# MLP 2's first pair all by Strassen's scheme, with VectorE's order written out and out tiles laid into their own batch's columns

## The chip, the cores and the metric

The kernel runs on one core of a Trainium2 chip. Its metric is the device time in microseconds. Before the change three runs took 769.46 to 769.73 us, median 769.64. An engine of the core works through its own queue in order: TensorE (matmuls, PE in the profile; its weight loads are PEld), VectorE (DVE), ScalarE (ACT), GpSimd (POOL) and SyncE (SP, which issues the DMAs). Engines wait for each other through semaphores.

## The reference, cut to what matters

Clustered attention feeds MLP 1 (512 to 2048 to 512, SiLU), and that feeds MLP 2, a gated one. The change is at the seam of the two MLPs.

```python
def _moe2_ref(x, w_gate, w_val, w_out):
    gate = 1.0 / (1.0 + np.exp(-(x @ w_gate)))
    val = x @ w_val
    return (gate * val @ w_out).astype(np.float32)
```

x has 1536 tokens (2 batches of 768) and 512 columns; MLP 2's hidden width is 1536. Everything is float32.

## The kernel before, in words

**Precision.** Every float32 operand is split into two tiles of a rounder type, hi and lo: ScalarE casts the source to hi (`cast`, L65), then VectorE or GpSimd subtracts hi from the source into lo (L77 for activations, L773 for weights, L956 in `split` for gated products). A product is three matmuls: hi hi, hi lo, lo hi.

**MLP 2 by pairs.** The hidden width is cut into six pairs of 256 columns (`i` from 0 to 5). Each pair has a gate weight (w2g), a value weight (w2v) and an out weight (w2o), each loaded as two chunks. A chunk is fetched raw (tiles rg, rv, ru; two buffers in all, so a fetch waits until the chunk two before it has been read for the last time), then converted: two ScalarE passes (L730, L732; tiles cg, cv, cu), one GpSimd pass (L733), two VectorE passes (L741, L748). `come` issues fetch and first passes, `arrive` the rest.

**Strassen's scheme** (`strassen`). The activations of a batch are four quarters b11, b21, b12, b22 (two row halves by two token halves of 384), the weight four quarters as well. Seven products with sums of the quarters replace eight: x, y, z, w, v, and X and W, which accumulate onto the banks of x and w. Each is six matmuls of 384 columns for one batch. X needs that ScalarE has copied x out of its bank (L923). The sums of the activations are t1 to t4 (L91 to L102), formed by VectorE and then split; those of the weight are formed by GpSimd (L793 to L796).

**The first pair.** It is the seam: MLP 1's last out products (`mixed`, tiles y, batch 0 then batch 1) are added to acc by VectorE (L996) while TensorE is to go on. In before, batch 0 of pair 0 is multiplied directly (`gated_directly`, tiles q and r, eight products with plain quarters), batch 1 by the scheme, gate first, then value; then come all six out tiles of pair 0 (`out_of(0)`, tiles z). An out tile is two blocks of 128 tokens by 512 columns (12 matmuls of 512 columns); pair 0's are copied by ScalarE into acc (L994), the later ones are added by VectorE. acc also holds MLP 1's result, the source of the quarters, so a tile may overwrite only columns whose quarters have been used. Tile z of blocks t and u goes to acc's columns t and u; those don't belong to one batch alone.

**Order.** TensorE's order is written out (a manual schedule), VectorE's, ScalarE's and GpSimd's are set by the scheduler, held back in places by `issue_after` (list `behind`).

## Time and profile before

| what | value |
|---|---|
| median of 3 runs | 769.64 us |
| profiled execution, its own time | 769.74 us |
| its span | 768.0 us |
| TensorE busy | 757.5 us (99%) |
| VectorE, ScalarE, GpSimd busy | 592.3, 425.2, 386.0 us |
| chain that ended last | TensorE 90%, VectorE 4%, ScalarE 3%, DMA 2% |

A timeline row gives the start in us from the span's start, the length, the engine, the source line, the operation, the tile written and those read. A matmul's own length (0.33 us for 384 columns) is longer than the distance to the next one, since they are pipelined; a block's cost is read from start to start. MLP 1's last out products run from 471.2 to 487.84, pair 0 of MLP 2 from there to 535.53, pair 1 begins there. In a name like g_1x the g is the gate (v: the value), 1 the batch, x the product; buffer numbers are left out.

### The profile page before, as it was taken

The numbers are of one execution on the slowest core, as the hardware profiler recorded it, in microseconds if no ns is written. First come the engines' busy times: TensorE is split into PE (matmuls) and PEld (weight loads), VectorE is DVE, ScalarE is ACT, GpSimd is POOL, SyncE is SP. The second block draws the span as 40 slices with busy tenths as digits, with TensorE's granted clock in tenths as the row PEclk, the third lists the DMA queues.
The fourth block names the chain that finished last, engine by engine and source line by source line (L and its number), as shares of the span: only waits on it lengthen the run. The fifth ranks groups of instructions, "written<-read, shape, count | busy, mean of one in ns | idle before, by whom it ended". The sixth has DMA issues, their size and how long they took to land.

```text
span 768.0 us, 11449 instructions
## 1 busy us (share of the span) xinstructions
PE 757.5 (99%) x4302; PEld 650.9 (85%) x4302; DVE 592.3 (77%) x762; ACT 425.2 (55%) x736; POOL 386.0 (50%) x359
## 2 busy tenths in 40 slices
PE   7999999999999999999999999999999999999997
PEld 4766776677768998998989989998998989999896
DVE  6887887788787968798978577966596767858566
ACT  6777776776886662544615536747434525353320
POOL 5335134643655772566646546355546745564430
PEclk9999999999999999999999999999999999999999
DMA  7677457447122122132222120111112112211104
GB/s 201 175 210 193 114 149 196 120 125 200 34 77 81 57 82 83 55 111 82 83 83 83 55 83 10 47 56 55 55 56 100 66 56 84 79 57 56 55 0 165
DMA packets 25487, 71.60 MB, mean 93 GB/s; under 512 B 4484, under 2 KB 4952, under 8 KB 25432
## 3 DMA queue, kind: packets, MB, share of 16 engines
q1 hardware_dynamic: 24888, 70.84, 30.8%
q8 instruction: 34, 0.56, 0.3%
q14 instruction: 21, 0.17, 0.1%
q10 hardware_dynamic: 544, 0.03, 0.0%
HBM read 48.01 MB, written 3.19 MB: 67 GB/s over the span
## 4 chain that ended last, share of the span: by engine, by line
PE 90%; DVE 4%; ACT 3%; DMA 2%; issue 1%; POOL 0%; SPq 0%; ACTq 0%; POOLq 0%; DVEq 0%
PE z L1078 12%; PE s L469 8%; PE v L519 7%; PE t L506 5%; PE y L1017 4%; PE h_0w L899 4%; PE h_0x L899 4%; PE g_0w L899 3%; PE g_0x L899 3%; PE v_0x L899 2%; PE v_0w L899 2%; PE y_00None L1017 2%; PE y_01None L1017 2%; PE y_20None L1017 2%; PE y_11None L1017 2%; PE y_10None L1017 2%
## 5 line engine op out<-in xcount | busy, mean ns | idle before, releaser
L482 ACT ACTIVATE e<-s,nm 128x768 f32<-128x768 f32 x96 | 86.4, 900 | 34.0 <-DVE nm L477 33.1
L477 DVE TENSOR_REDUCE nm<-s 128x1 f32<-128x768 f32 x96 | 91.4, 953 | 10.2 <-PE s L469 8.6
L1078 PE MATMUL z<-wu,ghb 128*128 128x512 f32 (+1 forms) x292 | 89.3, 387 | 0.7 <-DVE v_0u L913 0.7
L519 PE MATMUL v<-ph,vv 128*64 128x384 f32 x384 | 69.0, 494 | 0.2 <-DVE xf L531 0.2
L1078 PEld LDWEIGHTS z<-wu,ghb 128*128 128x128 f32 x292 | 54.4, 188 | 12.0 <-DVE v_0u L913 1.1
L469 PE MATMUL s<-ka,qa 128*128 128x384 f32 x192 | 57.5, 380 | 1.7 <-ACT e L482 1.3
L506 PE MATMUL t<-ident,e 128*128 128x128 f32 x384 | 58.5, 275 | 0.1
L996 DVE TENSOR_TENSOR acc<-z,acc 128x1024 f32<-128x1024 f32 (+2 forms) x32 | 37.0, 1157 | 26.7 <-PE z L1078 26.2
L1078 PE MATMUL z<-wu,glb 128*128 128x512 f32 (+1 forms) x146 | 56.5, 387 | 0.0
L506 PEld LDWEIGHTS t<-ident,e 128*128 128x128 f32 x384 | 44.9, 140 | 11.3 <-issue 9.0
L519 PEld LDWEIGHTS v<-ph,vv 128*64 128x64 f32 x384 | 24.7, 136 | 32.8 <-issue 29.0
L469 PE MATMUL s<-k,q 128*128 128x384 f32 x192 | 49.6, 339 | 0.0
L65 ACT ACTIVATE ph<-t 128x512 f32<-128x512 f32 x68 | 40.5, 597 | 12.4 <-PE t L506 11.8
L68 DVE COPY ph<-u 128x512 f32<-128x512 f32 x48 | 32.8, 683 | 16.3 <-PE u L496 16.3
L550 POOL TENSOR_TENSOR acc<-xf,rb 128x768 f32<-128x768 f32 x7 | 12.9, 1839 | 57.0 <-DMA rb<-d_rb 41.2
L773 POOL TENSOR_TENSOR wo<-co,wo 128x512 fp32r<-128x512 f32 x16 | 22.6, 1416 | 35.3 <-ACT wo L65 35.2
L773 POOL TENSOR_TENSOR wu<-cu,wu 128x512 fp32r<-128x512 f32 x12 | 15.5, 1295 | 42.1 <-ACT wu L65 42.1
L469 PEld LDWEIGHTS s<-k,q 128*128 128x128 f32 x192 | 34.5, 188 | 0.5 <-ACT k L339 0.3
L469 PEld LDWEIGHTS s<-ka,qa 128*128 128x128 f32 x192 | 28.9, 190 | 6.9 <-ACT e L482 6.0
L1017 PE MATMUL y<-gha,wo 128*128 128x384 f32 x128 | 32.8, 334 | 0.0
L1078 PEld LDWEIGHTS z<-wu,glb 128*128 128x128 f32 x146 | 27.4, 188 | 5.7 <-DVE glb L956 0.2
L531 DVE TENSOR_TENSOR xf<-v,other 64x384 f32<-64x384 f32 x32 | 17.7, 553 | 14.8 <-ACT other L528 14.3
(691 smaller groups left out, 2138.9 us busy)
## 6 DMA issues: line engine op xcount, KB each, us to landing
ri<-in_w1i SPq DMA_DIRECT2D x16, 512.0 KB, 3.2
ro<-in_w1o SPq DMA_DIRECT2D x16, 512.0 KB, 3.3
ka<-kh SPq DMA_DIRECT2D x32, 192.0 KB, 3.5
rg<-in_w2g SPq DMA_DIRECT2D x12, 512.0 KB, 4.1
rv<-in_w2v SPq DMA_DIRECT2D x12, 512.0 KB, 3.2
ru<-in_w2o SPq DMA_DIRECT2D x12, 512.0 KB, 3.2
qq<-in_qT SPq DMA_DIRECT2D x8, 384.0 KB, 3.4
kk<-in_kT SPq DMA_DIRECT2D x8, 384.0 KB, 4.2
```

The source lines that it names most:

```text
L65: return nc.scalar.activation(o, i, AF.Copy)
L68: return nc.vector.tensor_copy(o, i)
L469: nc.tensor.matmul(s[:, g, 0:HS], lhsT=a[:, j, i * P : (i + 1) * P], rhs=c[:, j, g * HS : (g + 1) * HS], start=n == 0, stop=n == 1,)
L477: maxima.append(nc.vector.tensor_reduce(nm, s[:, :, 0:HS], axis=AX.XY, op=ALU.max, negate=True))
L482: x = nc.scalar.activation(e, s[:, :, 0:HS], AF.Exp, bias=nm, scale=1.0, accum_out=tots[p][:, n : n + 1])
L506: nc.tensor.transpose(t[:, kt, :], e[:, kt * P : (kt + 1) * P], ident)
L519: m = nc.tensor.matmul(o[(L, U)[kt % 2]], lhsT=vv[:, j, kt, :], rhs=ring[:, kt, g * G : (g + 1) * G], start=n < 2, stop=n >= NT - 2,)
L773: nc.gpsimd.tensor_tensor(lo, src, hi, op=ALU.subtract)
L899: nc.tensor.matmul(o[:, b, 0:HS], lhsT=w[a][s][:, k, :], rhs=right[b, q][t][:, k, :], start=start and k == 0 and n == 0, stop=k == KQ - 1 ...
L996: added.append(nc.vector.tensor_tensor(z, o, z, op=ALU.add))
L1017: nc.tensor.matmul(o[:, d, 0:width], lhsT=s[:, d, k, :], rhs=t[:, c], start=k == 0 and m == 0, stop=k == 1 and m == 2,)
L1078: nc.tensor.matmul(o[:, a, c], lhsT=s[:, q * P : (q + 1) * P], rhs=r[:, c], start=k == 0 and m == 0, stop=k == 1 and m == 2, skip_group_ch ...
```

## The change

- Batch 0 of pair 0 goes by the scheme too. Gate and value products alternate in the order x X y z w v W (`together`), and ghb and glb of their products are split a little later (`late`).
- Out tiles of pair 0 are made of blocks of one batch and laid into that batch's columns (`place_of`), so three come after batch 0's products and three after batch 1's. In the later pairs a tile is made of the two batches' blocks. The rows stored at the end are reassembled by the store, from runs of 256 or 128 columns.
- From MLP 1's last out products to the end of batch 1's blocks VectorE's order is written out too. The conversions of w2o (pair 0), w2g and w2v (pair 1) are placed in it. ScalarE's sigmoid table is loaded by a tiny operation ahead of batch 0.

```diff
...
+    def scheme_operands(temporary, name, b, caster, adder):
+
+        b11, b21, b12, b22 = quarters(b).values()
+        sums = {}
+
+        def minus(n, x, y):
+            sums[n] = temporary(f"{name}t{n}{b}")
+            adder.tensor_tensor(sums[n], x, y, op=ALU.subtract)
+
+        def make(*which):
+            for w in which:
+                if w == "T1":
+                    minus("t1", b12, b11)
+                elif w == "T2":
+                    minus("t2", b22, sums["t1"])
+                elif w == "T3":
+                    minus("t3", b22, b12)
+                elif w == "T4":
+                    minus("t4", sums["t2"], b21)
+                elif w in sums:
+                    right_operand(name, b, w, sums[w], caster, adder)
+                else:
+                    right_quarter(name, b, w, caster, adder)
+
+        return make
...
+        if key[2:]:
+            chunk = result(coming[what, i].pop(0))
+            name = f"{what[1]}{i}"
+            if what == "2o":
+                made[place[key]] = two(chunk, f"u{i}_{key[2]}")
+            elif key[2]:
+                made[place[what, i]] = scheme(halves.pop(), chunk, name)
+            else:
+                halves.append(chunk)
...
-        for c in range(n, min(n + look[0] + 1, place["2o", 1, 0])):
+        for c in range(n, min(n + look[0] + 1, place["2o", 0, 0])):
...
-                if c == place["2g", 1]:
-                    behind.extend(multiplied[1:2] * 4 + multiplied[-1:] * 4)
...
+            parts = partial(split, g, m, (h, bs), f"b{i}", eng)
+            if together and eng is nc.vector:
+                late.append(parts)
+            else:
+                parts()
+
+        if together:
+            order = "xXyzwvW"
+            g = strassen(weights("2g", i), f"g{i}", gate, bs, order)
+            v = strassen(weights("2v", i), f"v{i}", value, bs, order)
+            for stage in (g, v) * 7:
+                next(stage)
+                yield
+            return
...
-    def gated_directly(i, b):
...
+    def place_of(t, u):
+
+        (h, b, r), (g, a, q) = t, u
+        if h != g:
+            return acc[:, :, :, b, half:].rearrange("p (g d) h s -> p g (d h) s", g=2)
+        if b == a:
+            return acc[:, 2 * h : 2 * h + 2, :, b, 0:half]
+        if r < 2:
+            return acc[:, 2 * h + r, :, :, 0:half].rearrange("p h b s -> p b h s")
+        return acc[:, 2 * h : 2 * h + 2, :, :, half:].rearrange("p d h b s -> p b (d h) s")
...
-        pairs = [(t, t + 1) for t in range(0, 2 * half, 2)]
         if i == 0:
-            ts = [t for b in range(B) for t in range(2 * half) if t % half // PER == b]
-            pairs = [tuple(ts[n : n + 2]) for n in range(0, 2 * half, 2)]
-        oc = oa.rearrange("p (t c) -> p t c", c=NB)
-        def products(o, t, u, k, rows=(0, 1), c=slice(0, NB)):
+            pairs = [p for b in range(B) for p in (((0, b, 0), (0, b, 1)), ((0, b, 2), (1, b, 2)), ((1, b, 0), (1, b, 1)))]
+        else:
+            pairs = [((h, 0, r), (h, 1, r)) for h in range(2) for r in ((0, 1, 2), (2, 0, 1))[h]]
...
+            accumulate(z, o.rearrange("p a (n w) -> p a n w", w=z.shape[-1]), i == 0)
...
+            nc.sync.dma_start(out[n : n + P, c].rearrange("t (n w) -> t n w", w=z.shape[-1]), z)
...
-    beside = plain_operands("y", 0)
-    steps(mixed(N1 - 1, 1), beside)
-    run(beside)
-    for q in ("11", "21", "22"):
-        right_quarter("y", 1, q, ACT, DVE)
-    run(sums("y", 1))
-    last("y", 1)
-    run(gated_directly(0, 0))
-    run(gated(0, ONE[1]))
-    run(sums("y", 0))
-    last("y", 0)
-    run(out_of(0))
+    come("2o", 0)
+    order.__exit__(None, None, None)
+    order = tc.manual_schedule(engines={mybir.EngineType.PE, mybir.EngineType.DVE})
+    order.__enter__()
+    zero, one = (scheme_operands(temporary, "y", b, ACT, DVE) for b in range(B))
+    rest = mixed(N1 - 1, 1)
+    zero("11", "21")
+    table = temporary("table")[:, 0, 0:1]
+    nc.scalar.activation(table, right[0, "21"][0][:, 0, 0:1].bitcast(F32), AF.Sigmoid)
+    zero("T1", "T2", "T3", "t2")
+    next(rest)
+    zero("t1", "T4")
+    next(rest)
+    next(rest)
+    zero("t3")
+    run(rest)
+    zero("t4")
+    arrive("2o", 0, 0)
+
+    def split_late():
+        while late:
+            late.pop(0)()
+
+    def both(b, between):
+        stages = gated(0, ONE[b], True)
+        for n in range(14):
+            next(stages)
+            if n in (4, 12, 13):
+                split_late()
+            for make, *what in between.get(n, ()):
+                make(*what)
+
+    both(0, {5: [(zero, "22")], 7: [(arrive, "2o", 0, 1), (come, "2g", 1)], 9: [(one, "11")]})
+    outs = out_of(0)
+    steps(outs, n=3)
+    one("21", "T1", "T2")
+    arrive("2g", 1, 0)
+    one("t2", "t1", "T3", "t3", "T4")
+    both(1, {5: [(one, "t4")], 7: [(one, "22")], 9: [(arrive, "2g", 1, 1), (come, "2v", 1)]})
+    order.__exit__(None, None, None)
+    order = tc.manual_schedule(engines={mybir.EngineType.PE})
+    order.__enter__()
+    arrive("2v", 1)
+    run(outs)
...
```

The instructions stand as follows in the built programs (line numbers of each kernel's own file; the number behind a name tells buffers apart).

TensorE, where batch 0 of pair 0 ends and batch 1 begins, before (r is the value of batch 0 formed directly, its six-matmul rows one per quarter):

```order
L966 MATMUL r_01_5384<-y_5195,wv0b 128x384 x6
L966 MATMUL r_01_5384<-y_5212,wv0b 128x384 x6
L966 MATMUL r_01_5384<-y_5229,wv0b 128x384 x6
L966 MATMUL r_01_5384<-y_5246,wv0b 128x384 x6
L899 MATMUL g_1x<-y_5249,wg0a 128x384 x6
L899 MATMUL g_1y<-yt_5262,wg0s 128x384 x6
L899 MATMUL g_1z<-yt_5272,wg0t 128x384 x6
L899 MATMUL g_1w<-yt_5275,wg0s 128x384 x6
L899 MATMUL g_1x<-y_5252,wg0a 128x384 x6
L899 MATMUL g_1v<-yt_5267,wg0b 128x384 x6
```

TensorE, the start of batch 0 now:

```order
L932 MATMUL g_0x<-y_5196,wg0a 128x384 x6
L932 MATMUL v_0x<-y_5196,wv0a 128x384 x6
L932 MATMUL g_0x<-y_5199,wg0a 128x384 x6
L932 MATMUL v_0x<-y_5199,wv0a 128x384 x6
L932 MATMUL g_0y<-yt_5210,wg0s 128x384 x6
L932 MATMUL v_0y<-yt_5210,wv0s 128x384 x6
L932 MATMUL g_0z<-yt_5260,wg0t 128x384 x6
L932 MATMUL v_0z<-yt_5260,wv0t 128x384 x6
L932 MATMUL g_0w<-yt_5227,wg0s 128x384 x6
L932 MATMUL v_0w<-yt_5227,wv0s 128x384 x6
```

The 16 rows of q and r have become 14 that alternate, and X comes two rows behind its x where it came four behind before.

ScalarE, around the copy of g_1x (the first product of batch 1), before:

```order
L1051 ACTIVATE g_1_0_5341<-q_01_5316 128x768
L65 ACTIVATE ghb_0_5380<-g_0_0_5314 128x2x384
L923 ACTIVATE g_1u_5415<-g_1x 128x384
L65 ACTIVATE ghb_1_5410<-g_1_0_5341 128x2x384
L65 ACTIVATE wg1d<-cg_1_5574 128x256
L65 ACTIVATE wg1a<-cg_0_5566 128x512
L1032 ACTIVATE g_001_5456<-g_1x 128x384
L730 ACTIVATE cv_0_5605<-rv_0_5603 128x512
L732 ACTIVATE rv_0_5603<-rv_0_5603 128x512
```

ScalarE there now (z_2 is the last out tile of batch 0; cv and rv are the passes over w2v's first chunk of pair 1, yt is the cast of t3 of batch 1):

```order
L65 ACTIVATE wg1a<-cg_0_5366 128x512
L1027 ACTIVATE acc<-z_2_5469 128x4x256
L756 ACTIVATE cv_0_5623<-rv_0_5621 128x512
L758 ACTIVATE rv_0_5621<-rv_0_5621 128x512
L65 ACTIVATE yt_5500<-ytt_5498 128x768
L956 ACTIVATE g_1u_5506<-g_1x 128x384
L956 ACTIVATE v_1u_5515<-v_1x 128x384
L1065 ACTIVATE g_001_5529<-g_1x 128x384
```

The two passes stood behind g_1x's copy and the sigmoid of its bank; now they and a cast stand ahead of the copy.

VectorE, where w2g's first chunk of pair 1 (cg_0) is converted, before (in before it runs beside batch 1's blocks):

```order
L1055 TENSOR_TENSOR g_0_0_5314<-r_00_5354,g_0_0_5314 128x768
L956 TENSOR_TENSOR glb_0_5381<-g_0_0_5314,ghb_0_5380 128x2x384
L1055 TENSOR_TENSOR g_1_0_5341<-r_01_5384,g_1_0_5341 128x768
L741 SCALAR_TENSOR_TENSOR cg_0_5566<-cg_0_5566,rg_0_5564 128x512
L741 SCALAR_TENSOR_TENSOR cg_1_5574<-cg_1_5574,rg_1_5572 128x512
L748 SCALAR_TENSOR_TENSOR cg_0_5566<-rg_0_5564,cg_0_5566 128x512
L913 TENSOR_TENSOR g_1u_5415<-g_1y,g_1u_5415 128x384
```

VectorE there now, at the end of batch 0 (glb and g_0u belong to batch 0's gated products, y and ytt to batch 1's operands):

```order
L989 TENSOR_TENSOR glb_1_5397<-g_0u_5341,ghb_1_5396 128x384
L946 TENSOR_TENSOR v_0u_5295<-v_0w,v_0u_5295 128x384
L1071 TENSOR_TENSOR g_0u_5286<-v_0u_5295,g_0u_5286 128x384
L989 TENSOR_TENSOR glb_0_5327<-g_0u_5286,ghb_0_5326 128x384
L77 TENSOR_TENSOR y_5483<-acc,y_5483 128x768
L113 TENSOR_TENSOR ytt_5486<-acc 128x768
L113 TENSOR_TENSOR ytt_5488<-acc,ytt_5486 128x768
L767 SCALAR_TENSOR_TENSOR cg_0_5366<-cg_0_5366,rg_0_5364 128x512
L774 SCALAR_TENSOR_TENSOR cg_0_5366<-rg_0_5364,cg_0_5366 128x512
```

The chunk's passes stand at the end of batch 0's work and of three operations for batch 1, and ahead of the rest of batch 1's operands.

## Rows read from the trace of the kernel before

**Rows 1.** The page: engine totals, and the granted clock over the span.
```profile
PE 757.5 (99%) x4302; PEld 650.9 (85%) x4302; DVE 592.3 (77%) x762; ACT 425.2 (55%) x736; POOL 386.0 (50%) x359
...
PEclk9999999999999999999999999999999999999999
```

**Rows 2.** Windows: length, busy us of PE, PEld, DVE, ACT, POOL, clock, DMA.
```profile
0.00:10.00 10.00, 7.23 (x30) 2.64 (x30) 6.10 (x43) 5.45 (x10) 2.92 (x10) 1.00 0.60 160
471.20:487.84 16.64, 16.64 (x97) 16.64 (x97) 15.75 (x18) 10.46 (x18) 8.89 (x9) 1.00 0.19 63
487.84:504.48 16.64, 16.64 (x97) 16.64 (x97) 13.99 (x16) 10.02 (x13) 3.48 (x3) 1.00 0.01 1
504.48:519.07 14.59, 14.59 (x85) 14.43 (x84) 9.90 (x17) 8.19 (x16) 10.36 (x11) 1.00 0.23 74
519.07:535.53 16.46, 16.46 (x73) 13.63 (x73) 12.61 (x18) 12.03 (x19) 7.50 (x7) 1.00 0.19 64
535.53:750.00 214.47, 214.10 (x1141) 201.85 (x1139) 150.19 (x153) 91.89 (x143) 114.18 (x114) 1.00 0.17 60
```

**Rows 3.** TensorE's timeline: start, length, engine, line, operation, tiles, count.
```profile
487.84 4.32 PE L966 MATMUL q<-y,wg0a 128*128 128x384 f32 x24
...
521.93 0.62 PE L1078 MATMUL z<-wu,ghb 128*128 128x512 f32 x2
...
524.65 0.62 PE L1078 MATMUL z<-wu,ghb 128*128 128x512 f32 x2
...
535.53 2.27 PE L899 MATMUL g_0x<-y,wg1a 128*128 128x384 f32 x12
```

**Rows 4.** Timeline of VectorE and GpSimd (fields as before).
```profile
478.14 0.95 DVE L77 TENSOR_TENSOR y<-acc,y 128x768 fp32r<-128x768 f32 x1
479.00 0.94 DVE L996 TENSOR_TENSOR acc<-y,acc 128x768 f32<-128x768 f32 x1
479.87 1.33 DVE L77 TENSOR_TENSOR y<-acc,y 128x768 fp32r<-128x768 f32 x1
...
505.56 1.28 DVE L741 SCALAR_TENSOR_TENSOR cg<-cg,rg 128x512 int32<-128x512 int32 x2
...
507.36 0.55 DVE L913 TENSOR_TENSOR g_1u<-g_1y,g_1u 128x384 f32<-128x384 f32 x1
...
479.10 1.29 POOL L773 TENSOR_TENSOR wu<-cu,wu 128x512 fp32r<-128x512 f32 x1 [3.36 <-ACT wu L65]
```

**Rows 5.** Timeline where h_0x's second product waits for ScalarE's copy.
```profile
441.32 0.49 ACT L923 ACTIVATE h_0u<-h_0x 128x384 f32<-128x384 f32 x1
...
441.86 1.32 PE L899 MATMUL h_0x<-x,wi7a 128*128 128x384 f32 x6
...
443.02 1.21 PE L899 MATMUL h_0z<-xt,wi7t 128*128 128x384 f32 x6
```

**Rows 6.** A chunk's transfer: VectorE's release, the issue, ScalarE's start.
```profile
477.54 0.68 DVE L748 SCALAR_TENSOR_TENSOR cu<-ru,cu 128x512 int32<-128x512 int32 x1
...
478.28 0.33 SPq L724 DMA_DIRECT2D rg<-in_w2g  x1
...
481.55 0.67 ACT L730 ACTIVATE cg<-rg 128x512 f32<-128x512 f32 x1 [0.72 <-DMA rg<-in_w2g]
```

**Rows 7.** ScalarE's timeline: conversion passes, a sigmoid, casts.
```profile
510.82 0.68 ACT L730 ACTIVATE cv<-rv 128x512 f32<-128x512 f32 x1
511.41 0.66 ACT L732 ACTIVATE rv<-rv 128x512 int32<-128x512 uint32 x1
511.96 0.51 ACT L1032 ACTIVATE g_1d<-g_1d 128x384 f32<-128x384 f32 x1
...
518.58 0.85 ACT L65 ACTIVATE yt<-yt 128x768 fp32r<-128x768 f32 x1 [2.65 <-DVE yt L91]
519.34 0.51 ACT L65 ACTIVATE ghb<-g 128x384 fp32r<-128x384 f32 x1
```

**Rows 8.** DMA issues of the end: KB each, median us to landing.
```profile
out<-acc SPq DMA_DIRECT2D x2, 128.0 KB, 2.4
```

More of the change, by code (lines that the diff above doesn't have):

```diff
@@ L796, in scheme @@
         sub(t[:, 3], a12, t[:, 1], op=ALU.subtract)
-        after = latest if name == "i0" else ()
+        after = latest if all_four else ()
         s12 = two(t[:, 0:2].rearrange("p a b -> p (a b)"), f"{name}s", after=after)
@@ L827, in clustered_attention_then_two_mlps @@
     for i in range(N2):
-        job(("2g", i), seven, [flat(w2g[2 * i + n]) for n in range(2)], f"g{i}", i == 0)
-        job(("2v", i), seven, [flat(w2v[2 * i + n]) for n in range(2)], f"v{i}", i == 0)
+        job(("2g", i), seven, [flat(w2g[2 * i + n]) for n in range(2)], f"g{i}")
+        job(("2v", i), seven, [flat(w2v[2 * i + n]) for n in range(2)], f"v{i}")
         for k in range(2):
             job(("2o", i, k), plain, flat(w2o[2 * i + k]), f"u{i}_{k}")
-    coming = {}
+    coming, halves = {}, []
     def come(*key):
@@ L840, in come @@
         if what == "2o":
-            coming[key] = [begun([flat(w2o[2 * i + k])], f"u{i}_{k}", True) for k in range(2)]
+            coming[key] = [begun([flat(w2o[2 * i + k])], f"u{i}_{k}", True)[0] for k in range(2)]
         else:
@@ L850, in arrive @@
             return
-        if what == "2o":
-            for k, chunks in enumerate(coming.pop(key)):
+        if key[2:]:
[7 more added lines that the diff above has]
+                halves.append(chunk)
+        elif what == "2o":
+            for k, chunk in enumerate(coming.pop(key)):
                 behind.extend(critical[-1:] * 2)
-                made[place["2o", i, k]] = two(result(chunks[0]), f"u{i}_{k}")
+                made[place["2o", i, k]] = two(result(chunk), f"u{i}_{k}")
         else:
@@ L946, in clustered_attention_then_two_mlps @@
     gs = {}
-    parted, multiplied = [], []
+    parted, multiplied, late = [], [], []
     def split(src, m, at, i, subber):
@@ L1025, in mixed, with gated @@
                 yield
-    def gated(i, bs):
+    def gated(i, bs, together=False):
         gates = {}
@@ L1043, in gated @@
         yield from strassen(weights("2g", i), f"g{i}", gate, bs)
         yield from strassen(weights("2v", i), f"v{i}", value, bs)
-    def gated_directly(i, b):
-        gates = {}
-        def gate(c, m, b):
-            gates[m] = temporary(f"g2{i}_{m}_{b}")
-            nc.scalar.activation(gates[m], c, AF.Sigmoid)
-        def value(c, m, b):
-            g = gates[m]
-            multiplied.append(nc.vector.tensor_tensor(g, c, g, op=ALU.mult))
-            split(g, m, (slice(0, 2), b), f"b{i}", nc.vector)
-        yield from direct(weights("2g", i), f"q{i}", gate, b)
-        yield from direct(weights("2v", i), f"r{i}", value, b)
@@ L1073, in products @@
+        def products(o, tu, k, rows=(0, 1), c=slice(0, NB)):
             fh, fl = f[k]
@@ L1115, in out_of @@
             if i == N2 - 1 and n == len(pairs) - 1:
-                last_products(n, *some[0])
+                last_products(n, some[0])
                 return
-            banks = [bank(f"z{i}_{t}", third(n + c, i in (0, N2 - 1))) for c, (t, _) in enumerate(some)]
+            banks = [bank(f"z{i}_{n + c}", third(n + c, i in (0, N2 - 1))) for c in range(len(some))]
             for k in range(2):
                 for o, tu in zip(banks, some):
-                    products(o, *tu, k)
+                    products(o, tu, k)
                     if k == 1:
-                        evict(o, *tu)
+                        evict(o, tu)
                         yield
```

44 lines of the change are left out of this document (18 added, 26 removed).

## The prediction

> **What bounds the kernel now.** I read the page's first parts, then the stretches around MLP 2's first pair, then each engine's timeline there. TensorE is busy 757.5 of 768.0 us, its granted clock is full in every slice, and from MLP 1's last out tiles to the end of MLP 2's first pair it is busy without a gap [rows 1, 2]. So a matmul that goes is worth its whole time, and a wait that comes in costs its whole time: between 535.53 and 750 TensorE is idle 0.37 us in all [rows 2], so nothing later gives a delay back. VectorE, ScalarE and GpSimd are off the path and count where TensorE waits for them.
>
> **The removed matmuls.** Batch 0's gate and value products are now formed directly: 96 matmuls of 384 columns in 16.64 us (487.84 to 504.48). By the scheme, as batch 1 has it, there are 14 blocks of six: 14.59 us (504.48 to 519.07), 1.04 a block, 12 matmuls less, -2.05 us [rows 2]. An out tile takes 2.72 us (521.93, 524.65) [rows 3]; the six of before took 16.46 [rows 2], 0.14 more than six times that. Without waits the new stretch is 14.59 + 8.16 + 14.59 + 8.16 = 45.50 us; it took 47.69 (487.84 to 535.53) [rows 3]. **-2.2 us**, and pair 1 would begin at 533.3. The rest asks what TensorE will wait for.
>
> **Entry: no wait.** MLP 1's last two out stages take 16.64 us for eight groups [rows 2], so the third is there at 471.2 + 3 x 2.08 = 477.44. From it VectorE has in its written order 15 operations 0.87 us apart (479.00, 479.87) and a chunk's two conversion passes, 1.28: 477.6 + 13.05 + 1.28 = 491.9 [rows 4]. The first that TensorE waits for afterwards is the add of g_0y, due before g_0z at 487.84 + 6 x 1.04 = 494.08, and it can't start before g_0y ends (493.2). About 1 us may slip unseen. The conversion of u, in before among these adds, now stands behind them, and GpSimd's next weight waits for it; so nothing on GpSimd slows VectorE there, as it did before (a subtraction of 0.95 us took 1.33 beside it, 479.87) [rows 4].
>
> **Where X waits for ScalarE.** In the order xXyzwvW the product X accumulates onto x's bank and waits until ScalarE has copied x out; one block of 1.04 us lies between (v's x). Before has this shape once. ScalarE was late, its copy ran from 441.32 for 0.49, X began at 441.86, and the block behind it at 443.02, 1.16 later instead of 1.04, since the weights weren't loaded ahead [rows 5]. So X starts 0.05 after the copy's end, and a wait adds 0.12. In batch 0 ScalarE's casts are done by 488.1 (VectorE's sixth add by 487.2, a cast of 0.85 [rows 7]), and x ends at 489.04: no wait.
>
> **Batch 1: the wait that decides.** Between the eviction of z_2 and the copy of g_1x ScalarE's queue now holds the two conversion passes of w2v's first chunk (cv, rv) and the cast of t3. The passes need the transfer, the transfer needs the raw buffer that VectorE's second pass of w2g's first chunk (cg) frees, and that stands behind batch 0's last products and three operations on batch 1's operands. Step by step:
> - v_0z ends at 487.84 + 8 x 1.04 + 0.16 = 496.32; VectorE's add (0.55, the next 0.08 sooner) and two passes (1.28) [rows 4]: 498.1. That frees the buffer for w2g's second chunk. From VectorE's end to the issue 0.06 us (478.22, 478.28), from there to ScalarE's start on the landed chunk 3.27 (481.55) [rows 6]: 501.44.
> - ScalarE: 0.59 + 0.55 for its two passes, 0.43 for one cast of 384 columns, 0.51 to the end of the next (ghb of m = 1) [rows 7]: 503.5. TensorE wants it for z_0's second half, loaded at 502.43 + 1.36 - 0.19 = 503.6: no wait. The low part (VectorE, 0.55) is 0.1 to 0.45 us late.
> - VectorE from 503.57: this low part, an add, a multiply, then, after a cast, the low part of m = 0, to 506.2; the low part of batch 1's quarter 21, T1 and T2 at 0.87, and cg's two passes, 1.28: 510.05. If the first of these is slowed by 0.38, as the subtraction at 479.87 was [rows 4], 510.4.
> - Issue and landing 3.33: 513.4 to 513.8. ScalarE: 0.59, 0.55, 0.76 (the cast of t3, 0.85 long), 0.49 for the copy [rows 5 to 7]: 515.8 to 516.2.
> - X was to start at 502.43 + 8.16 + 2.08 = 512.67. It is 3.2 to 3.55 late, with the reload 3.3 to 3.65. Waits ahead of it (z_0's low part; v_1x, whose bank z_2's eviction frees) are inside this, since the transfer sets an absolute time. I take **+3.5**: GpSimd's own low part falls just there.
>
> On that choice the Trainium skill has a rule (GPSIMD Engine Reference, "8. Key points"): GpSimd shares its memory interfaces with VectorE and contends with VectorE instructions that have two SBUF inputs. The trace agrees: an add out of PSUM kept its 0.94 us beside GpSimd (479.00), a subtraction of two SBUF tiles behind it took 1.33 [rows 4]. By the rule the wait is 3.65, without it 3.3.
>
> **Batch 1's end.** The second chunk of w2v goes the same way. Call the end of batch 1's blocks E. v_1w ends at E - 4.0; VectorE's add and cg's two passes: E - 2.2; the transfer, 3.33: E + 1.1. ScalarE then makes its two passes (1.14), a cast for wg1s (0.55) and only then the ghb that z_4's second tile loads (0.51): E + 3.3, or 3.65 where GpSimd's sums for wg1s are late. TensorE wants it at E + 2.72 + 0.68 - 0.19 = E + 3.2. With the low part behind it and the reload 0.2 to 0.7: **+0.5**.
>
> **What costs nothing.** The weights need less: of the second chunk of w2g and w2v 256 columns are split instead of 512. ScalarE's table load stands between two casts whose sources come 2 us apart. VectorE's evictions into runs of 256 and 128 columns aren't shown; two runs of 384 (479.00) took no longer per column than the rest [rows 4], and from 535.53 to 750 VectorE is busy 150 of 214 us [rows 2]. Pair 1's weight s is split near E + 5, and needed at E + 10.7. The output leaves in pieces of 1 KB and 512 B instead of 2 KB; the two stores that already have 1 KB rows land in 2.4 us [rows 8], and the last one keeps its shape. Between 0 and +0.3 us through a fuller queue; I take +0.05.
>
> **Sum.** -2.2 + 3.5 + 0.5 + 0.05 = +1.85 us on the profiled execution's own 769.74 us (0.1 above the median of 769.64): **771.6 us**. By the low ends (3.3 and 0.2): 771.0; by the high ends (3.65 and 0.7), with 0.6 for GpSimd slowing VectorE in the y and z blocks too, where each bank must drain within 1.04 us, and 0.3 at the end: 772.8.
>
> **Rivals.**
> 1. Everything is hidden: the transfer lands before z_2 is evicted and ScalarE isn't held. Only -2.2 counts: 767.5. For it: nothing in before's stretch made TensorE wait. Against: the transfer can't be issued before 508.7 even if ScalarE never waited in batch 0 (v_0w ends at 502.56; its add, multiply, cast and low part take it to 504.9, the five behind 3.8).
> 2. The hold is shorter: VectorE does reach cg at 508.7. Landing 512.0, copy done 514.4, X 1.9 late with the reload, batch 1's end 0.2: -0.1 us, 769.6. For it: each step rests on the one before, so a cast that comes early carries through.
> 3. The slower side: a stop of two to three microseconds lowers TensorE's clock, from a wait of about 2 us on. At 1.2 GHz a block of 1.04 us would take 2.08; no row here is at that level. Two blocks: +2.1, 773.7. Against it: in the first 10 us TensorE is idle 2.8 us, and the granted clock is 1.00 there [rows 2]. The Trainium skill (TensorE: Matmul & The Clock Gate, "Part 1: The HAM clock gate") says that an idle TensorE falls back to the lower clock; no run here shows it.
>
> **Chances.** My sum 0.55, rival 1 0.13, rival 2 0.17, rival 3 or further waits 0.15. A change under 0.2% (1.5 us, 768.1 to 771.2) can't be told from none. Faster is rival 1: 0.13. Within: rival 2 and the low fifth of my sum: 0.27. Slower: 0.60. The range is 769.2 to 773.2 (my sum's own 771.0 to 772.8); it leaves out rival 1 and most of rival 3.
>
> **What would show it.** TensorE's longest wait in this stretch is at batch 1's second g block, for ScalarE's copy of g_1x, and ScalarE stands idle ahead of its cv pass until w2v's chunk lands; a smaller wait is in the fifth out tile. I am wrong if the cv pass finds its chunk landed (767.5), or if the granted clock falls below 1.00.

## The result, and the profile after

Four runs after took 777.4 to 779.23 us, median 778.89; four of before on the same chip 769.27 to 769.73, median 769.55. The ratio is 1.0118 (95% interval 1.0100 to 1.0136): 9.3 us slower, where 771.6 was forecast. The profiled execution took 779.23 us, its span is 777.5. TensorE is busy 761.0 us against 757.5 [rows 1], though 12 matmuls are gone (13 records fewer): some of them ran slower.

The stretch from batch 0's first block to pair 1, in windows (length; busy us of PE, PEld, DVE, ACT, POOL; granted clock; DMA share), cut at batch 0's blocks, its out tiles, g_1x and v_1x with the stop, the second products of x, batch 1's other blocks, its out tiles, the later pairs:

```profile
487.89:503.22 15.33, 15.03 (x85) 14.35 (x84) 14.84 (x22) 7.29 (x14) 4.89 (x4) 1.00 0.21 71
503.22:512.76 9.54, 8.77 (x37) 6.63 (x37) 7.62 (x12) 6.24 (x11) 1.63 (x2) 1.00 0.00 1
512.76:518.04 5.28, 2.54 (x13) 1.89 (x11) 3.97 (x4) 3.61 (x7) 2.15 (x2) 0.98 0.29 99
518.04:521.69 3.65, 3.65 (x12) 3.65 (x13) 1.43 (x2) 1.54 (x3) 0.00 (x0) 0.56 0.02 4
521.69:532.10 10.41, 10.41 (x61) 10.41 (x61) 9.16 (x15) 2.51 (x5) 2.63 (x3) 1.00 0.04 9
532.10:544.24 12.14, 10.57 (x38) 7.67 (x38) 9.25 (x10) 7.82 (x13) 11.99 (x12) 0.86 0.35 121
544.24:760.00 215.76, 215.09 (x1145) 202.72 (x1144) 151.79 (x155) 93.29 (x145) 115.38 (x115) 1.00 0.17 59
```

It took 56.35 us where 45.50 was computed without waits and 47.69 was before's [rows 3]. The last row but one against its 8.16, and the fourth against 2.08, have something besides waits in them: the clock, 0.86 and 0.56. From pair 1 to 760 TensorE is idle 0.67 us in 215.76 (before: 0.37 in 214.47 [rows 2]): nothing is given back, as forecast.

TensorE's waits from 484 to 560 (line waited for; us, times, longest), and the rows of its timeline around them:

```profile
PE g_1x L932 <- ACT g_1u L956: 2.7, 1, 2.7
PE z L1119 <- ACT ghb L65: 0.9, 1, 0.9
PE z L1119 <- ACT rg L758: 0.8, 1, 0.8
PE z L1119 <- DVE glb L989: 0.6, 1, 0.6
PE v_0z L932 <- DVE v_0u L946: 0.3, 1, 0.3
```

```profile
504.14 0.70 PE L1119 MATMUL z<-wu,ghb 128*128 128x512 f32 x2 [0.77 <-ACT rg L758]
...
512.76 1.23 PE L932 MATMUL g_1x<-y,wg0a 128*128 128x384 f32 x6
...
518.04 2.29 PE L932 MATMUL g_1x<-y,wg0a 128*128 128x384 f32 x6 [2.68 <-ACT g_1u L956]
520.12 1.73 PE L932 MATMUL v_1x<-y,wv0a 128*128 128x384 f32 x6
521.69 1.20 PE L932 MATMUL g_1y<-yt,wg0s 128*128 128x384 f32 x6
...
536.83 0.73 PE L1119 MATMUL z<-wu,ghb 128*128 128x512 f32 x2 [0.94 <-ACT ghb L65]
538.19 0.72 PE L1119 MATMUL z<-wu,glb 128*128 128x512 f32 x1 [0.63 <-DVE glb L989]
538.71 1.05 PE L1119 MATMUL z<-wu,ghb 128*128 128x512 f32 x2
```

Two blocks behind the long stop take 2.08 and 1.57 from start to start instead of 1.04; the pairs of out matmuls behind 538.19 take 0.85 instead of 0.46 (the row behind the pair of 538.71 starts at 539.56). The wait of z_0 is put down to ScalarE's rg pass, whose tile no matmul reads; z_0's bank is freed by VectorE's add of g_0w, which ended at 504.0 as well (503.45 and 0.55).

ScalarE ahead of the long stop's end:

```profile
512.96 1.03 ACT L1027 ACTIVATE acc<-z 128x1024 f32<-128x1024 f32 x1
515.65 0.68 ACT L756 ACTIVATE cv<-rv 128x512 f32<-128x512 f32 x1 [1.67 <-DMA rv<-in_w2v]
516.23 0.65 ACT L758 ACTIVATE rv<-rv 128x512 int32<-128x512 uint32 x1
516.78 0.83 ACT L65 ACTIVATE yt<-ytt 128x768 fp32r<-128x768 f32 x1
517.51 0.47 ACT L956 ACTIVATE g_1u<-g_1x 128x384 f32<-128x384 f32 x1
```

This is the order that the prediction named: two passes over w2v's chunk, behind its transfer, the cast of t3, and then the copy that X waits for. VectorE and GpSimd, which set these times (rows of both, on one clock; compare [rows 4]: 0.95 for a subtraction of 768 columns, 0.55 for an operation of 384):

```profile
499.91 2.01 DVE L77 TENSOR_TENSOR y<-acc,y 128x768 fp32r<-128x768 f32 x1
...
504.91 1.07 DVE L989 TENSOR_TENSOR glb<-g_0u,ghb 128x384 fp32r<-128x384 f32 x1 [0.91 <-ACT ghb L65]
...
511.63 0.69 DVE L774 SCALAR_TENSOR_TENSOR cg<-rg,cg 128x512 int32<-128x512 int32 x1
512.56 2.91 DVE L77 TENSOR_TENSOR yt<-ytt,yt 128x768 fp32r<-128x768 f32 x2 [0.24 <-ACT yt L65]
515.39 0.95 DVE L113 TENSOR_TENSOR ytt<-acc 128x768 f32<-128x768 f32 x1
...
499.81 1.29 POOL L799 TENSOR_TENSOR wu<-cu,wu 128x512 fp32r<-128x512 f32 x1 [2.28 <-ACT wu L65]
...
513.12 1.53 POOL L799 TENSOR_TENSOR wg1a<-cg,wg1a 128x512 fp32r<-128x512 f32 x1 [7.55 <-ACT wg1a L65]
```

The subtraction at 499.91 began 0.1 after GpSimd's and took 1.07 longer than alone; the two at 512.56 took 2.91 instead of 1.82. The cg pass (511.63) that frees the raw buffer for w2v's chunk ends at 512.32. So T3 (515.39) ends at 516.34, and even without the passes its cast could start only 0.44 sooner than it did.

### The profile page after: what moved, and what is told of

The parts are those of the page before. It is cut to its first block, busy times and chain, and to the rows that moved or that the text cites. A ratio compares the mean times of both kernels' runs of the same rounds, so it can differ in the third digit from the quotient of the medians.

```text
span 777.5 us, 11461 instructions
## 1 busy us (share of the span) xinstructions
PE 761.0 (98%) x4289; PEld 650.9 (84%) x4290; DVE 602.1 (77%) x773; ACT 426.6 (55%) x742; POOL 386.8 (50%) x361
## 4 chain that ended last, share of the span: by engine, by line
PE 85%; DVE 5%; ACT 4%; DMA 2%; issue 2%; POOL 1%; SPq 0%; ACTq 0%; POOLq 0%; DVEq 0%
PE z L1119 11%; PE s L495 8%; PE v L545 7%; PE t L532 5%; PE y L1050 4%; PE h_0w L932 4%; PE h_0x L932 4%; PE g_0x L932 3%; PE v_0x L932 3%; PE g_0w L932 3%; PE v_0w L932 2%; PE y_00None L1050 2%; PE y_21None L1050 2%; PE y_20None L1050 2%; PE y_11None L1050 2%; PE y_10None L1050 2%
```

## The experiments

Medians are of 4 runs, or 6 to 11 where that many were made; every ratio is to before's runs in the same job, whose median lay between 769.89 and 770.40. A table of the stretch comes behind the experiments. By its ratio after would take 779.0 to 779.5 us in these jobs.

### Filling the stops (e1_fill)

In both long stops TensorE was given matmuls whose result is overwritten.

```diff
+            if n == "X" and fill and name == "g0_1":
+                early["y"] = bank(f"{name}y")
+                filling(early["y"], w["a11"][0][:, 0, :], right[1, "11"][0][:, 0, :], 18)
...
+                    if fill and i == 0 and n == 4 and k == 0:
+                        products(o, tu, k, (0,))
+                        dummy = bank("z0_5", third(5, True))
+                        fh, wh = f[0][0], weights("2o", 0, 0)[0]
+                        for _ in range(6):
+                            nc.tensor.matmul(dummy[:, 0], lhsT=fh[:, 0:P], rhs=wh, start=True, stop=True)
+                        products(o, tu, k, (1,))
```

> The kernel after, with dummy matmuls in TensorE's two longest stops: 18 of 384 columns (about 2.9 us) ahead of batch 1's second g block, written into the bank that the y block then overwrites, and 6 of 512 columns (1.3 us) ahead of the second row of the fifth out tile, into the sixth's bank. No wait goes; only TensorE isn't idle in it. Theory (a stop lowers TensorE's clock, and the blocks behind it run at half speed): the granted clock stays 1.00 from 484 to 560, the blocks behind the stops take 1.04 us again; -3.2 us for the clock, +0.2 to +0.6 for dummies that outlast the waits: 775.9 to 776.4 against 778.9 of after. Rival (the clock falls for another reason, or the low rows in the trace cost nothing): 778.9 to 779.5.

Measured: 777.19 us, ratio 1.0092 (1.0077 to 1.0107). In its trace the granted clock is 1.00 from 484 to 560, here where it was low in after:

```profile
518.00:521.70 3.70, 3.70 (x23) 3.63 (x22) 1.90 (x3) 2.44 (x5) 0.00 (x0) 1.00 0.00 0
538.70:541.30 2.60, 2.60 (x13) 2.15 (x12) 2.21 (x2) 0.32 (x1) 2.60 (x3) 1.00 0.25 95
```

The stretch takes 53.50, 2.85 less, with no wait taken away. The theory's size holds for the profiled execution (1.54 and 1.59 of clock won, 0.29 lost to dummies that outlast the waits). Its time was missed: by the ratios the medians differ by 2.0, and the two intervals overlap. That the clock, and not only the waiting, costs time is shown by the rows: 2.85 us in the stretch, 2.0 by the medians.

### What holds ScalarE's copy (e2_hold_v0, e7_hold_both)

First the two passes alone were moved behind the copies of g_1x and v_1x, then T3 and t3 too. VectorE's order stays as it is in both.

```diff
+        keep = held.pop(name)[-1] if name in held else None
...
+            with tc.issue_after(keep.ins) if keep else nullcontext():
+                nc.scalar.activation(low, low.bitcast(mybir.dt.uint32), AF.Copy, scale=LAST)
...
+    held["v1_0"] = copies
...
-    one("t2", "t1", "T3", "t3", "T4")
+    one("t2", "t1")
+    def late_t3():
+        with tc.issue_after(copies[-1].ins):
+            one("T3", "t3", "T4")
```

(The lower part is of the second kernel alone; late_t3 is called behind v_1x, batch 1's second block.)

> The kernel after, with ScalarE's two conversion passes of w2v's first chunk (cv, rv) issued behind its copies of g_1x and v_1x; nothing else moves. Theory of the prediction (those two passes, and the transfer that they wait for, hold the copy): X starts without its wait of 2.7 us and the clock stays up there: -4.2 us, 774.7. Rival (what else stands ahead of the copy, the cast of t3, is as late: its source is VectorE's T3, done at 516.3, behind the low parts of t2 and t1): the copy would come at 517.1 instead of 517.5, the wait stays above 2 us and the clock falls all the same: 778.2 to 778.9.

> As e2_hold_v0, and batch 1's T3 and t3 are also made behind the two copies (on ScalarE; VectorE's order is unchanged). By both theories nothing late is left ahead of the copy: it runs when x is done and z_2 evicted (about 514), X starts at about 515.0 with no wait, the granted clock stays 1.00 there: -2.7 for the wait and -1.6 for the clock, 774.6. If a wait moves to a later block (t3 for z, the second chunk for out tile five), less: up to 776.5. Against it: if what holds TensorE there is the bank of v_1x (freed by z_2's eviction) and not the copy, the gain is under 1 us: 778.

The first: 777.98, ratio 1.0104 (1.0089 to 1.0119, which overlaps after's interval). The rival was right: with the passes gone the copy waits for the cast, which waits for VectorE, and TensorE's stop is 2.31 us instead of 2.68.

```profile
517.13 0.84 ACT L65 ACTIVATE yt<-ytt 128x768 fp32r<-128x768 f32 x1 [2.40 <-DVE ytt L113]
517.88 0.47 ACT L959 ACTIVATE g_1u<-g_1x 128x384 f32<-128x384 f32 x1
...
518.41 1.59 PE L935 MATMUL g_1x<-y,wg0a 128*128 128x384 f32 x6 [2.31 <-ACT g_1u L959]
519.79 2.12 PE L935 MATMUL v_1x<-y,wv0a 128*128 128x384 f32 x6
521.71 1.68 PE L935 MATMUL g_1y<-yt,wg0s 128*128 128x384 f32 x6
```

The clock falls here too (1.38, 1.92 and 1.52 from start to start for three blocks, 1.7 us lost), but not at the fifth out tile, though its waits of 0.93 and 0.64 us are there as in after. That second fall, 1.6 us, is nearly all of the 1.8 us that the stretch is shorter.

The second: 775.65, ratio 1.0072 (1.0057 to 1.0087), in the range that was expected. The stop is gone, and with it the low clock. A new one takes its place four blocks on, where the add of g_1y stands behind t3's low part and T4 on VectorE:

```profile
515.23 1.20 PE L935 MATMUL g_1x<-y,wg0a 128*128 128x384 f32 x6
...
520.70 1.31 PE L935 MATMUL g_1z<-yt,wg0t 128*128 128x384 f32 x6 [1.15 <-DVE g_1u L949]
```

So two holds of almost one length stood ahead of the copy. The forecast had priced the first and thought the second hidden by it; both hang on VectorE's order.

### The order of the blocks (e4_order)

Both batches in the order x y z w X v W, all of the gate and then all of the value. The first low part of each batch, split behind the fifth block in after, comes behind the twelfth, and three operands are split one to three blocks earlier.

```diff
-            order = "xXyzwvW"
+            order = "xyzwXvW"
...
-            for stage in (g, v) * 7:
+            for stage in (g,) * 7 + (v,) * 7:
```

> The kernel after, with pair 0's blocks in the order x y z w X v W, first all of g and then all of v, as batch 1 ran in before; the same matmuls, the operands written out in the same places but batch 1's t4 and 22 two and three blocks earlier. Rival that the interleaved order itself is at fault (X one block behind x): the stop before X goes, 774 to 775. Theory (batch 1's operands and the weights' transfers are late on VectorE's written order, whatever the order of the blocks): the stop goes from X to the z block, which then wants t3 (its low part is done at 518.6 in after) at about 514.8: a stop of 3 us or more there, and 777.5 to 780.

Measured: 786.04, ratio 1.0219 (1.0195 to 1.0243). The stop did move to the z block:

```profile
518.55 0.44 PE L932 MATMUL g_1z<-yt,wg0t 128*128 128x384 f32 x1 [2.66 <-ACT yt L65]
519.55 1.34 PE L932 MATMUL g_1z<-yt,wg0t 128*128 128x384 f32 x5 [0.55 <-DVE yt L77]
...
544.43 0.80 PE L1119 MATMUL z<-wu,glb 128*128 128x512 f32 x1 [3.45 <-DVE glb L989]
```

In after X began at 518.04, here z gets its operand at 518.55 and the rest of it at 519.55. That the time would stay within 780 was wrong: all multiplies and low parts now fall into batch 1's end, and the fifth out tile waits 3.45 us for one of them. Behind 2.66 and behind 3.45 the granted clock falls to 0.50 here too. The interleaved order by itself is not what costs the time, since the stop stays without it; it spreads VectorE's work.

### VectorE's order left to the scheduler (e12_free)

```diff
-    order = tc.manual_schedule(engines={mybir.EngineType.PE, mybir.EngineType.DVE})
+    order = tc.manual_schedule(engines={mybir.EngineType.PE})
```

> The kernel after with one part undone: VectorE's order in MLP 2's first pair is not written out but left to the scheduler; TensorE's order, the blocks and the operands stay. The scheduler moves w2g's and w2v's conversions some 15 to 20 us ahead (so that ScalarE's queue is not held by a transfer at the copy of g_1x) and batch 1's operands ahead of batch 0's last products. Theory (the written order puts the transfers where they hold ScalarE): the stop ahead of batch 1's second g block goes, and with it 4 us; in its place batch 0's out tiles wait for low parts that now stand behind batch 1's operands, 2 to 4 us: 776 to 779. Rival (the written order is better than the scheduler's in all): 780 or more.

Measured: 784.94, ratio 1.0190 (1.0176 to 1.0205); the rival. The stop ahead of X is gone in batch 1 (14.91 us for its blocks), but batch 0 takes 36.82 us where 22.75 was planned: v_0x waits 3.14 us, and z_0 3.07, for adds behind conversions and operands, two more waits are 1.62 and 1.19, and most of the other 5 us is the clock, at 0.50 behind the long ones.

```profile
492.62 1.82 PE L932 MATMUL v_0x<-y,wv0a 128*128 128x384 f32 x6 [3.14 <-DVE acc L1029]
...
512.55 0.70 PE L1119 MATMUL z<-wu,ghb 128*128 128x512 f32 x2 [3.07 <-DVE g_0u L946]
```

So a written order is worth having here; this one is not the best.

### One slowed subtraction moved (e9_move11)

Batch 1's quarter 11, whose subtraction took 2.01 us, was split behind batch 0's blocks.

```diff
-    both(0, {5: [(zero, "22")], 7: [(arrive, "2o", 0, 1), (come, "2g", 1)], 9: [(one, "11")]})
+    both(0, {5: [(zero, "22")], 7: [(arrive, "2o", 0, 1), (come, "2g", 1)]})
...
-    one("21", "T1", "T2")
+    one("11", "21", "T1", "T2")
```

> The kernel after, with batch 1's quarter 11 split after batch 0's blocks and not among them (the subtraction that took 2.01 us at 499.91 beside GpSimd, where 0.95 is its time alone). Theory: the wait of the first out tile (0.77, and the slip of 1.4 us over the three out tiles) goes, but the stop ahead of batch 1's second g block ends at a time that the chain cg passes, transfer of w2v, cv sets, and that chain starts only 0.4 to 0.9 us earlier (1.1 us of slowing gone, the order else the same): -0.4 to -0.9 us in all. Rival (batch 0's slip adds to the sum by itself): -1.4 us or more.

Measured: 779.15, ratio 1.0121 (1.0107 to 1.0134): no gain that can be told from after. Batch 0's blocks end 0.92 us sooner (15.33 from the first block to z_0 instead of 16.25), and the stop ahead of X grows by as much:

```profile
518.32 2.29 PE L932 MATMUL g_1x<-y,wg0a 128*128 128x384 f32 x6 [3.58 <-ACT g_1u L956]
```

The second product begins at 518.32 against 518.04. That the transfer sets an absolute time, as the prediction had it, is shown: time saved ahead of it turns into waiting. Even the 0.4 to 0.9 expected did not come: the moved subtraction still stands ahead of the cg passes on VectorE, they end at 512.56 instead of 512.32, and cv waits for its chunk until 515.94. The clock costs 2.5 us behind this longer stop instead of 1.57, and does not fall at the fifth out tile (1.6 us less), so these two cancel in part.

### The out layout (e3_layout, e8_rows)

Before with `place_of` and the new pairs alone; and after with its last sums written into free weight buffers as whole rows, so that stores have rows of 2 KB again.

```diff
-            accumulate(z, o.rearrange("p a (n w) -> p a n w", w=z.shape[-1]), i == 0)
+            if i < N2 - 1:
+                accumulate(z, o.rearrange("p a (n w) -> p a n w", w=z.shape[-1]), i == 0)
+                return
...
+                full = rp.tile([P, KD * P], mybir.dt.int64, tag="r", name=f"f{n}").bitcast(F32)
...
+            nc.vector.tensor_tensor(
+                full.rearrange("p a (n w) -> p a n w", w=w_), o.rearrange("p a (n w) -> p a n w", w=w_), z, op=ALU.add
+            )
+            for a, t in enumerate(tu):
+                store(t, full[:, a])
```

> The kernel before with one part of the change alone: out tiles laid into their own batch's columns, so that evictions write runs of 256 and 128 columns and the output leaves in pieces of 1 KB and 512 B. Theory (the stores' landing, 3.1 us in the middle and 4.7 at most in after against 2.4 in before, is the +0.77 between VectorE's last end and the end of the span): +0.5 to +0.9 us, the ratio to before 1.0006 to 1.0012, and all of it behind the last matmul. Prediction's figure: +0.05, ratio 1.000 to 1.0003. A rival by which the evictions themselves are slower would show as TensorE waiting for banks in the out stages of pairs 0 to 5: more than 1 us.

> The kernel after, whose last evictions write each out tile's sum into a tile of its own with whole rows (free weight buffers) instead of back into the batch's columns, so that stores have rows of 2 KB as in before; the rest is untouched. Theory: the tail goes back from 4.0 to 3.3 us, 778.9 to 778.1 (ratio about 0.001 lower than after's 1.0118). Rival (the longer tail is the state of the DMA queues or the last tile, not the pieces): unchanged.

The layout alone: 770.51, ratio 1.0008 (0.9999 to 1.0017), +0.6 us by the ratio, not told from nothing by its interval alone. In the traces the time from the start of VectorE's last sum to the end of the span is 3.67 in before, 4.22 with the layout, 4.44 in after, 3.52 with whole rows (777.87, ratio 1.0105, 1.0092 to 1.0119; the interval overlaps after's). What moves during the last stores (GB/s in 40 slices; before 757 to 766, after 766 to 775):

```profile
GB/s 337 400 392 373 373 391 355 419 355 401 400 355 55 0 0 0 0 164 364 391 401 364 400 246 0 0 0 0 0 191 364 373 401 373 391 364 382 410 323 351
...
out<-acc SPq DMA_DIRECT2D x7, 256.0 KB, 2.4
```

```profile
GB/s 260 5 5 9 14 18 23 200 341 341 360 328 341 360 289 273 316 291 289 255 328 294 285 257 328 291 271 289 287 291 326 325 360 351 323 360 350 333 346 341
...
out<-acc SPq DMA_DIRECT2D x9, 256.0 KB, 3.1
```

Rows of 2 KB move at 355 to 419 GB/s with pauses between out tiles, pieces of 1 KB at 320 to 360 and pieces of 512 B at 255 to 328, all without a pause: the queue no longer empties between out tiles, and the last store waits for the rest. The landing of a 256 KB store (3.1 us, in before 2.4) says the same. The evictions themselves cost nothing that TensorE sees: its last matmul starts at 763.97 with the layout and at 764.02 in before. The other traces agree but for two: 4.19 to 4.32 with pieces, 3.55 and 3.58 with whole rows, but 5.06 (pieces) and about 4.3 (whole rows) in the first and the third of the versions that follow. What lengthens those stays open. So +0.05 was too low; 0.5 to 0.8 is what the traces of before, the layout alone and after show.

### All of it at once (e10_all, e11_best, e13_best2, e14_best3)

From the traces a version was built with T2, T3 and their operands ahead of w2g's conversion, ScalarE's passes behind the casts and copies that TensorE waits for, the second conversion of w2g behind batch 1's last low part, and quarter 11 behind batch 0; then one with T4 and t1 ahead of batch 1 as well, w2v's second chunk behind pair 1's wg1t, and whole rows in the stores.

```diff
-    one("21", "T1", "T2")
-    arrive("2g", 1, 0)
-    one("t2", "t1", "T3", "t3", "T4")
-    both(1, {5: [(one, "t4")], 7: [(one, "22")], 9: [(arrive, "2g", 1, 1), (come, "2v", 1)]})
+    one("11", "21", "T1", "T2", "T3", "t2", "T4", "t3", "t1")
+    arrive("2g", 1, 0)
...
+    both(1, {5: [(one, "t4")], 7: [(one, "22")], 9: [(come_v,)], 13: [(arrive, "2g", 1, 1)]})
+    held["v1_1"] = [wcasts["g1t"]]
+    come("2v", 1, 1)
```

(This is the second; the first has t3's operands ahead of the conversion, t1 and T4 among the blocks.)

> The kernel after with all of what the traces point to: quarter 11 split behind batch 0; T2, T3 and their operands ahead of w2g's conversion on VectorE; ScalarE's passes over w2g's second chunk behind batch 0's casts, over w2v's chunks behind batch 1's copies and casts; w2g's second conversion behind batch 1's last low part; the first low part of the gate behind v_y's add. The same arithmetic and the same matmuls. Theory (the loss is made up of waits of TensorE for ScalarE and VectorE that stand in an order that the transfers upset, and of the clock behind these): TensorE's waits between 487.9 and pair 1 fall to 0.5 to 2 us, the granted clock is 1.00, the stretch takes 46 to 48 us instead of 56.3: 769 to 771. Rival (VectorE and GpSimd haven't the time: other waits take their place): above 773.

> The kernel of e10_all with what its trace showed left: T4 and t1 of batch 1 made ahead of its blocks (one g_1z wait of 1.6 us for an add that stood behind T4), w2v's second chunk and the split of wv1a held behind pair 1's wg1t (a wait of 0.9 us for wg1s), and the last sums written into tiles with whole rows, as in e8_rows. Theory: the stretch from batch 0's first block to pair 1 takes 46 to 47 us against 47.7 in before and 56.3 in after, no wait of over 0.5 us is left, the tail is 3.4 us: 768.0 to 770.0, the ratio to before 0.998 to 1.000. Rival (VectorE is too full between 505 and 518 for any order): a wait of 1 us or more for one of batch 1's operands or adds, 771 or more.

The first: 773.76, ratio 1.0049 (1.0034 to 1.0065). TensorE has two waits left, 1.6 us at g_1z and 0.9 in pair 1. The waits in the stretch are as the theory had them, but its time, 769 to 771, was missed and the rival's bound, 773, is met; 1.4 us of what it lacks to before lies in the end of the kernel (5.06 against 3.67). The second: 769.89, ratio 0.9996 (0.9987 to 1.0005), no longer to be told from before. From batch 0's first block to pair 1 it takes 46.90 us, 0.8 less than before, the clock full (windows from g_1x to pair 1, then all its waits of the stretch):

```profile
511.52:526.00 14.48, 14.03 (x81) 13.70 (x80) 12.12 (x19) 7.61 (x13) 3.39 (x4) 1.00 0.10 37
526.00:535.04 9.04, 9.04 (x42) 7.60 (x41) 5.98 (x10) 3.88 (x6) 3.31 (x5) 1.00 0.20 65
```

```profile
PE v_1x L940 <- ACT acc L1035: 0.4, 1, 0.4
PE z L1127 <- ACT ghb L65: 0.2, 1, 0.2
```

What is missing of the 0.8 went into pair 1, whose first out tile waits 0.61 us (573.05) for a low part that before had in time. Two variants meant to win it back did not:

> e11_best with w2g's second conversion back among batch 1's blocks (after stage 9, as in after) and w2v's second chunk and wv1a held behind wg1s instead of wg1t, so that pair 1's later weights and passes come some 4 us sooner. Theory (what e11_best still loses, 0.6 us at pair 1's first out tile and some tenths behind it, comes from the passes and splits that were pushed into pair 1, where GpSimd slows VectorE): that wait goes, 769.0 to 769.6, the ratio to before 0.998 to 0.9995. Rival: the conversion among the blocks and GpSimd's sums beside it slow batch 1's last multiplies and low parts, and the wait in out tile four or five is back: 770 to 771.

> e11_best with one hold placed earlier: w2v's second chunk and the split of wv1a wait for wg1s instead of wg1t; VectorE's order among the blocks is e11_best's. Theory (0.6 us of e11_best is a wait at pair 1's first out tile that comes of passes pushed into pair 1): the wait goes and none comes in, since batch 1's end is as in e11_best: 769.2 to 769.8, the ratio to before 0.9980 to 0.9995. Rival: wg1t's split, now behind cv and wv1a, comes late for pair 1's z block, 0.5 to 1.5 us: 770 to 771.

The first: 772.71, ratio 1.0033 (1.0021 to 1.0046), the rival's wait, though 1.7 us above its range: ScalarE's last cast of batch 1 again stands behind wg1s, and the fifth out tile waits for it. The second: 770.89, ratio 1.0010 (1.0001 to 1.0019); its stretch is the shortest, 46.76, but pair 1's z block waits 0.91 us for wg1t, as its rival said.

```profile
531.35 0.73 PE L1127 MATMUL z<-wu,ghb 128*128 128x512 f32 x2 [1.59 <-ACT ghb L65]
```

```profile
540.92 1.66 PE L940 MATMUL g_0z<-yt,wg1t 128*128 128x384 f32 x8 [0.91 <-POOL wg1t L802]
```

No version here beats before by more than its interval.

### The stretch in the kernels with the scheme in both batches

Us from start to start in the profiled execution: batch 0 (g_0x to g_1x, three out tiles in it), batch 1's blocks (to z_3), its out tiles (to pair 1). The first row is the plan without waits.

| kernel | batch 0 | batch 1's blocks | its out tiles | sum |
|---|---|---|---|---|
| no waits | 22.75 | 14.59 | 8.16 | 45.50 |
| after | 24.87 | 19.34 | 12.14 | 56.35 |
| stops filled | 24.86 | 18.07 | 10.57 | 53.50 |
| passes held | 24.88 | 19.10 | 10.56 | 54.54 |
| passes and t3 held | 24.91 | 16.66 | 10.52 | 52.09 |
| quarter 11 moved | 24.42 | 21.22 | 10.53 | 56.17 |
| order x y z w X v W | 25.79 | 20.00 | 16.75 | 62.54 |
| VectorE by the scheduler | 36.82 | 14.91 | 9.57 | 61.30 |
| all at once, first | 23.18 | 16.86 | 8.20 | 48.24 |
| all at once, second | 23.38 | 15.32 | 8.20 | 46.90 |
| all at once, third | 23.23 | 15.32 | 10.87 | 49.42 |
| all at once, fourth | 23.24 | 15.32 | 8.20 | 46.76 |
| after, whole rows in the stores | 24.88 | 20.62 | 10.52 | 56.02 |

## Why the prediction was wrong

The profiled execution's balance, in the prediction's terms: -2.2, then 56.35 - 45.50 = 10.85 of waits and clock where 4.0 was forecast, 0.05 ahead of the stretch and 0.77 at the end where 0.05 was: +9.48 together, and from 769.74 to 779.23 it is 9.49. Of the 7.6 us above the 771.6 forecast, the clock is 3.2 (forecast 0), the time until batch 1's second product 1.8 (5.3 for 3.5), batch 1's end 1.9 (2.4 for 0.5) and the end of the kernel 0.7.

- **The removed matmuls: right.** A block takes 1.04 in after as well, and with the waits out the stretch came to 46.76 and 46.90, 1.3 and 1.4 above the computed 45.50, of which 0.45 and 0.65 are waits; the rest, 0.8, is not accounted for.
- **Entry: right.** g_0x begins 0.05 later than q did. The first wait comes eight blocks on, 0.3 us at v_0z, for an add behind a low part that took 1.28 instead of 0.55 beside GpSimd (494.02).
- **The place and the mechanism of the wait: right.** The longest wait is at batch 1's second g block, for the copy of g_1x, with ScalarE idle ahead of cv until the chunk landed; a smaller one is in the fifth out tile.
- **The size of batch 1's wait: the step that failed first.** "VectorE from 503.57 ... 510.05", with 0.38 as the most that GpSimd would add. The cg passes ended at 512.3, 2.3 later. The loss starts in batch 0: the subtraction at 499.91 lost 1.07 and the low part at 504.91 lost 0.5, each beside GpSimd, and ScalarE's two passes over w2g's second chunk (502.85 to 504.06 in the chain) stood ahead of ghb. The second product of x began at 518.04; the plan had 512.67 + 0.05 for the entry, so 5.3 instead of 3.5. That the trace of before had one slowed subtraction (0.38) was taken as the size; the one that started just behind GpSimd's lost nearly all that was left of it. The Trainium skill says so (SBUF — State Buffer, "SBUF: two separate sides"): of an operation of GpSimd and one of VectorE with two SBUF inputs, whichever starts first gets the shared ports for its whole instruction, and the other blocks. The trace agrees: 1.07 lost, with 1.19 of GpSimd's operation left.
- **That the conversion passes hold the copy was half of it.** With them out the copy still came at 517.88, by the start of the stretch (0.73 later in that trace) only 0.36 sooner; T3 and t3, which the sum counted as 0.76 of ScalarE's time, are late by themselves, for the slowed subtractions at 512.56. This rival was not in the forecast.
- **Batch 1's end: 0.5 forecast, 2.4 measured** (10.52 to 10.57 in the kernels with the same order and a full clock there, 8.16 without waits). The chunk landed at E + 1.8 (533.87) and not E + 1.1, since the second cg pass took 1.39 instead of 0.69 beside GpSimd (529.33). Then wg1s waited for a sum of GpSimd's, which took 1.19 instead of 0.74 beside VectorE, and the multiply ahead of ghb and the low part behind it took 1.09 and 1.08 instead of 0.56 and 0.55. Both engines slowed each other where the sum had them alone.
- **The clock: the largest term, rival 3, which was given 0.15 with others and put at nothing in the sum.** It happened, twice in the profiled execution: 1.57 and 1.6 us, 3.2 in all. The price of a block at half speed (2.08 for 1.04) was right, the two whole blocks per fall were not. The evidence against it was misread. The 2.8 us of idling in the first 10 us of before are several stops, none longer than 1.3 us, and though that window is given a clock of 1.00, its rows are not at full speed: the first matmuls of 512 columns start 0.43 us apart (weight loads at 2.15, 2.58, 3.00, 3.43), the later ones 0.22 (two rows below). So "no row here is at that level" does not hold, and the 1.00 there was no evidence. The mean clock of the four runs is 0.995, 0.996, 0.996 and, in the one of 777.4 us, 0.997, as in the kernel with the passes held, which had one fall; this fits one fall in that run, which no profile shows. The Trainium skill (TensorE: Matmul & The Clock Gate, "Part 1: The HAM clock gate") says that an idle TensorE falls back to half speed; the traces agree, 0.50 behind a stop of 2.31 us.

```profile
1.72 3.53 PE L211 MATMUL pw<-wt 128*128 128x512 bf16 x9
...
8.23 1.89 PE L211 MATMUL pw<-wt 128*128 128x512 bf16 x8
```

- **The end: +0.05 forecast, +0.77 measured**, of which the layout alone shows 0.55 (4.22 against 3.67).

The range was too narrow for a reason that can be named: each wait was priced with its neighbours at their undisturbed lengths, and errors along one chain (VectorE, transfer, ScalarE, TensorE, clock) add up instead of averaging out.

## What to carry to other kernels

An instruction on an in-order engine that waits for a transfer holds everything behind it, so place it behind what the bounding engine needs next, and look for the second hold behind the first: taking one away shows the other, and here only both together gave the time back. Price an operation of VectorE with two SBUF inputs by its length plus what may be left of a GpSimd operation that started before it, and let a stop of TensorE as long as the ones here (2.31 us and more) count once for itself and once for the clock behind it, which cost 1.6 to 2.9 us here. Look at the distance between matmuls, too, before taking a window's clock for full. A saving of 2 us in matmuls is less than one such chain cost.
